# Attention, a gated layer and a rational layer in one kernel: sums of weights and tokens on GpSimd, the second layer's conversion spread over blocks 1 to 8, another order of VectorE's work in the pairs' stage

## The chip, the core and the metric

One core of a Trainium2 chip runs the whole program. The metric is the device time of one execution in microseconds, the median of several. TensorE (PE) multiplies, VectorE (DVE), ScalarE (ACT) and GpSimd (POOL) work on tiles, and SyncE (SP) issues nearly all transfers. Each engine, and SP's queue, works in the order in which the program issues to it.

## What is computed

Eight batches of eight heads attend over keys and values that are averaged in groups of eight; the result, 4608 tokens of 512 values, goes through a gated layer of 1536 hidden values, and then through a layer of 2048 with a rational function. In float32:

```
k_p, v_p = mean of k, v over 8 neighbours              # 576 -> 72 rows
x  = softmax(q @ k_p.T / 8) @ v_p                      # 4608 x 512
y  = (silu(x @ w_gate) * (x @ w_val)) @ w_out          # hidden 1536
h  = y @ w_in                                          # 2048
out = ((a0 + a1 h + a2 h^2 + a3 h^3) / (1 + |b0||h| + |b1| h^2 + 1e-6)) @ w_out2
```

## The kernel before

**Splitting.** A product in float32 is made of three products of rounded parts: every operand is split into a high part (ScalarE copies it into the rounded type) and a low part (VectorE subtracts the high part from the value). `split` (line 92) does both. The weights come as 64-bit numbers and are first converted to float32 in pieces: two ScalarE instructions (`words`), three VectorE ones and one integer addition on GpSimd (`bits`, lines 114 to 121), then the split.

**Stages.** Tokens are worked on in nine blocks of 512. The head does the attention of block 0. Blocks 0, 1 and 2 (the plain blocks, loop `for j in range(PLAIN)`) do the gated layer in 12 steps `f` of 128 hidden values: gate product, value product, their elementwise product, output product of the step before. In block 0 the first layer's weights are converted alongside. Then come three pairs of blocks (3 and 4, 5 and 6, 7 and 8), 36 steps `n`, in the pairs' stage. There Strassen's scheme takes 7 products of half-sized operands in place of 8 for the hidden values; a chain of banks `ca`, `cb`, `cc` accumulates them. The parts a11, s1, s2, a12, s3, s4, a22 of the weights are streamed from DRAM two steps ahead (`stream`), and the parts b11, t1, t2, b21, t3, b22, t4 of the tokens are made once per pair (`token_sums`, line 657, and `token_part`). The hidden values go to DRAM. A product stage then applies the output weights to the three pairs, again with 7 products (banks `ya`, `yb`, `yc`, line 1025), and the second layer runs over all nine blocks.

**Sums of the weights.** `weight_sums` runs in blocks 1 and 2, half a step's weights at a time: `whole` (line 607) adds the two parts of a weight, `sums` (612 to 615) makes four sums, `parts` splits them and stores them, all on VectorE and ScalarE. The same for the output weights is `out_load`, `out_sums` (803 to 810) and `out_parts`, in the steps of the third pair: two tiles of 512 KB are loaded back from DRAM per step, six VectorE instructions work on them, and 1 MB is split and stored.

**The second layer's weights.** `Halves` converts 64 pieces of 256 columns: `load`, then `step`, which starts one piece (ScalarE), finishes the one before it on VectorE and GpSimd, splits and stores the one before that. All of it stands in the pairs' stage. `rate(n)` gives the calls of `step` in step `n`: one and two in turn up to step 23, one up to 30, five from step 31 to 35.

**Order around the change.** The order is written out by hand. In a step of the pairs' stage TensorE does s1, s2, [place A: transposes of the attention], a22 of the step before (`end_chain`), a12, [place B: values], s4, a11 of the next step (`begin_chain`), s3, [place C: scores]. On VectorE the addition at line 876 stands behind `second.step()` and place A; the addition at 905 ends the step. TensorE's s4 needs the first, its a22 the second. `attention_slots` puts the attention of later blocks into these places: the softmax's scaling at line 372 and the copies of p at 383 run on GpSimd for pairs' blocks, and the transposes (line 400) need both. In block 2 these are the units of blocks 3 and 4, in steps 0 to 9. `prepare(2)` loads K and V pieces and reduces them at the end of the same step.

## Time and profile before

| | us |
|---|---|
| median of 3 runs | 1963.39 (1961.37 to 1963.74) |
| the profiled execution | 1963.66 |
| its span | 1961.9 |
| TensorE busy | 1813.9 |
| VectorE busy | 1484.3 |
| ScalarE busy | 1135.0 |
| GpSimd busy | 195.7 |

The span runs from the first to the last instruction of the profiled execution; the rows below are from that execution, with times counted from the span's start. By these times block 1 runs from 193 to 308 us, block 2 to 443, the pairs' steps from there to 953, the product stage to about 1155, and the second layer to the end. A wait in a view is idle time of an engine, put down to what released it; the chain follows the waits back from the last instruction.

### The profile page before, as it was taken

What the parts mean: (1) busy time and instruction counts of PE and PEld (TensorE: products, weight loads), DVE (VectorE), ACT (ScalarE), POOL (GpSimd) and SP (SyncE); (2) the same over time, 40 slices, a digit from 0 to 9 for tenths busy, and PEclk for the clock granted to TensorE, in tenths of its full rate; (3) what the DMA queues carried; (4) which work ended last, traced back from release to release, by engine and by line L of the source; (5) the groups of instructions that cost most, each with busy time, mean ns of one, the idle gap of its engine ahead of it and who ended that gap; (6) DMA issues with size and microseconds to landing.
All of it is one profiled execution on the core that took longest, in us unless ns stands there. A gap on an engine that the chain in (4) does not pass through costs nothing.

```text
span 1961.9 us, 23800 instructions
## 1 busy us (share of the span) xinstructions
PE 1813.9 (92%) x8212; PEld 1436.3 (73%) x8212; DVE 1484.3 (76%) x2563; ACT 1135.0 (58%) x1972; POOL 195.7 (10%) x258
## 2 busy tenths in 40 slices
PE   6889999998988998774899999999999999999998
PEld 5667777876776777653577778888888888888887
DVE  8997676675667556653676679898988888898987
ACT  5675345546555654332444467666767676766675
POOL 3563001201211220001000000000000000000000
PEclk9999999999999999987899999999999999999999
DMA  6521545477878777997972570101010010101000
GB/s 244 199 95 46 174 137 177 169 266 269 276 257 268 256 260 252 383 324 271 311 266 110 194 257 1 43 1 43 1 44 27 17 43 1 43 1 44 1 22 22
DMA packets 157464, 285.27 MB, mean 145 GB/s; under 512 B 12320, under 2 KB 78496, under 8 KB 156320
## 3 DMA queue, kind: packets, MB, share of 16 engines
q1 hardware_dynamic: 156192, 282.64, 41.9%
q8 instruction: 65, 1.06, 0.2%
q10 hardware_dynamic: 1152, 1.12, 0.2%
q14 instruction: 55, 0.45, 0.1%
HBM read 194.58 MB, written 89.13 MB: 145 GB/s over the span
## 4 chain that ended last, share of the span: by engine, by line
PE 67%; DVE 16%; DMA 9%; issue 4%; ACT 3%; SPq 1%; POOL 0%; POOLq 0%; ACTq 0%; DVEq 0%
PE acco L246 20%; PE h L246 20%; PE ca L246 5%; PE vp L246 4%; PE cc L246 3%; PE ya L1025 3%; PE acc L246 2%; PE gp L246 2%; DMA oo<-od 2%; PE cb L246 2%; PE pv L428 1%; PE yb L1025 1%; PE yc L1025 1%; DVE p L360 1%; DVE vp L293 1%
## 5 line engine op out<-in xcount | busy, mean ns | idle before, releaser
L246 PE MATMUL acco<-wo,gt 128*128 128x512 f32 x1728 | 426.6, 395 | 2.7 <-ACT gt L1112 2.2
L246 PE MATMUL h<-z,wi 128*128 128x512 f32 x1728 | 423.1, 393 | 0.8 <-ACT z L93 0.8
L246 PEld LDWEIGHTS acco<-wo,gt 128*128 128x128 f32 x1728 | 325.2, 188 | 80.6 <-ACT gt L1112 3.1
L246 PEld LDWEIGHTS h<-z,wi 128*128 128x128 f32 x1728 | 324.4, 188 | 77.0 <-ACT z L93 1.6
L1091 ACT ACTIVATE sq<-h 128x512 f32<-128x512 f32 x144 | 86.1, 598 | 221.4 <-PE h L246 221.3
L1098 DVE SCALAR_TENSOR_TENSOR w<-sq,neg,w 128x512 f32<-128x512 f32 x144 | 108.2, 751 | 66.7 <-ACT w L1092 62.2
L246 PE MATMUL gp<-x,wg 128*128 128x512 f32 x432 | 110.9, 404 | 10.3 <-POOL wg L149 10.3
L1108 DVE SCALAR_TENSOR_TENSOR g<-t,neg,e 128x512 f32<-128x512 f32 x144 | 108.3, 752 | 5.1
L1095 ACT ACTIVATE t<-h,neg 128x512 f32<-128x512 f32 x144 | 111.9, 777 | 0.0
L246 PE MATMUL vp<-x,wv 128*128 128x512 f32 x432 | 111.5, 406 | 0.3
L1104 DVE SCALAR_TENSOR_TENSOR t<-t,neg,h 128x512 f32<-128x512 f32 x144 | 107.7, 748 | 5.1
L246 PE MATMUL ca<-x2t,sw 128*128 128x512 f32 x216 | 62.5, 430 | 50.5 <-DVE cq L905 50.5
L1105 DVE SCALAR_TENSOR_TENSOR e<-w,ln 128x512 f32<-128x512 f32 x144 | 98.8, 686 | 13.5 <-ACT ln L1102 13.4
L246 PE MATMUL acc<-ht,wo 128*128 128x512 f32 x432 | 106.9, 396 | 0.4 <-ACT ht L732 0.4
L1102 ACT ACTIVATE ln<-ln,lnb 128x512 f32<-128x512 f32 x144 | 104.2, 724 | 4.7
L1106 DVE SCALAR_TENSOR_TENSOR e<-e,ln 128x512 f32<-128x512 f32 x144 | 99.7, 692 | 5.0
L246 PEld LDWEIGHTS gp<-x,wg 128*128 128x128 f32 x432 | 80.2, 190 | 31.4 <-POOL wg L149 13.0
L1112 ACT ACTIVATE gt<-g 128x512 fp32r<-128x512 f32 x144 | 91.0, 632 | 16.8 <-DVE g L1108 16.8
L1113 DVE TENSOR_TENSOR gt<-g,gt 128x512 fp32r<-128x512 f32 x144 | 98.9, 687 | 1.5 <-ACT gt L1112 0.8
L1092 ACT ACTIVATE w<-h,cab 128x512 f32<-128x512 f32 x144 | 98.3, 682 | 2.5 <-DVE e L1105 2.4
L1103 DVE TENSOR_TENSOR t<-t,h 128x512 f32<-128x512 f32 x144 | 98.3, 682 | 0.0
L246 PEld LDWEIGHTS vp<-x,wv 128*128 128x128 f32 x432 | 81.8, 194 | 20.1 <-POOL wv L149 2.1
(244 smaller groups left out, 3160.4 us busy)
## 6 DMA issues: line engine op xcount, KB each, us to landing
sw<-sd SPq DMA_DIRECT2D x72, 512.0 KB, 6.8
sw<-wd SPq DMA_DIRECT2D x36, 512.0 KB, 5.5
h<-hq SPq DMA_DIRECT2D x36, 512.0 KB, 3.5
sd<-sp SPq DMA_DIRECT2D x24, 512.0 KB, 3.2
sw<-vd SPq DMA_DIRECT2D x36, 256.0 KB, 7.2
hl<-h SPq DMA_DIRECT2D x18, 512.0 KB, 7.8
hr<-h SPq DMA_DIRECT2D x18, 512.0 KB, 9.9
out<-ob SPq DMA_DIRECT2D x36, 256.0 KB, 2.3
```

The source lines that it names most:

```text
L246: nc.tensor.matmul(acc, st[:, lw, cols], mv[:, rw, mcols], start=first and i == 0, stop=last and i == n - 1, skip_group_check=seeded,)
L1025: nc.tensor.matmul(banks[q], w[:, lw, cols], t[:, rw, :], start=opened and k == 0 and m == 0, stop=k == NK - 1 and m == 2, skip_group_chec ...
L1092: nc.scalar.activation(w0, hps, AF.Abs, scale=cab[:, 4:5])
L1095: nc.scalar.activation(t, hps, AF.Identity, scale=neg[:, 3:4], bias=neg[:, 2:3])
L1098: nc.vector.scalar_tensor_tensor(w0, sq, neg[:, 5:6], w0, op0=ALU.mult, op1=ALU.add)
L1102: nc.scalar.activation(ln, ln, AF.Exp, scale=-1.0, bias=lnb)
L1103: nc.vector.tensor_tensor(t, t, hps, op=ALU.mult)
L1104: nc.vector.scalar_tensor_tensor(t, t, neg[:, 1:2], hps, op0=ALU.add, op1=ALU.mult)
L1105: nc.vector.scalar_tensor_tensor(e, w0, C1, ln, op0=ALU.add, op1=ALU.mult)
L1106: nc.vector.scalar_tensor_tensor(e, e, 2.0, ln, op0=ALU.subtract, op1=ALU.mult)
L1108: nc.vector.scalar_tensor_tensor(g, t, neg[:, 0:1], e, op0=ALU.add, op1=ALU.mult)
L1113: lambda gt=gt, g=g: nc.vector.tensor_tensor(gt[:, 1, :], g, f32(gt[:, 0, :]), op=ALU.subtract),
```

## The change

- `split` can subtract on GpSimd. `weight_sums` does all its sums and its subtraction there; its store is issued at the next step.
- `out_load` goes. `out_sums` runs in block 2, steps 3 to 8, on the weights in SBUF, and `out_parts` and `out_store` follow, with sums and subtraction on GpSimd.
- `Halves` is cut into `begin`, `middle` and `end`: one piece is begun, converted, split (on GpSimd) in each step of blocks 1 and 2 and of the pairs, two in the last four steps, and stored at the next step's `begin`. Loads lead by one step. The pieces lie in three buffers of their own, in the pairs' stage in those of x too.
- `token_sums` and the sums of `hidden_part` in the product stage run on GpSimd.
- In a step of the pairs' stage the addition at line 876 is issued ahead of place A; `token_part` of t1 and t2 and the conversion come behind `end_chain`; the hidden values are stored one step later; K and V are reduced a step after they are loaded, ahead of place B.
- `vp` has one buffer in place of two, and the DMA scratch 1024 bytes in place of 4096.

```diff
-    def split(dst_hi, dst_lo, src):
+    def split(dst_hi, dst_lo, src, eng=None):
         nc.scalar.activation(dst_hi, src, AF.Copy)
-        nc.vector.tensor_tensor(dst_lo, src, f32(dst_hi), op=ALU.subtract)
+        (eng or nc.vector).tensor_tensor(dst_lo, src, f32(dst_hi), op=ALU.subtract)
...
+                i, self.n = self.n % 7, self.n + 1
+                if self.paired and i < KT:
+                    t = keep.tile([P, 2, BLK], F32R, tag=f"x{i}", name=f"raw{key}_{h}")
+                    t = t.rearrange("p t c -> p (t c)")
+                else:
+                    t = hp.tile([P, 768], F32R, tag="cv", name=f"raw{key}_{h}", bufs=3)
...
+        def store(self):
+            for key, h, w in self.after:
+                nc.sync.dma_start(self.kept[key][:, :, h * 256 : (h + 1) * 256], f32(w))
+            self.after = []
+
+        def begin(self, n=1, more=1):
+            self.store()
+            for _ in range(more):
+                self.load()
+            self.now = []
+            for key, h, tile_, raw in [self.raw.pop(0) for _ in range(min(n, len(self.raw)))]:
+                t = f32(tile_[:, 512:768])
                 words, bits, _ = conversion(f"{key}_{h}", raw, 256, True, t)
                 words()
+                self.now.append((key, h, tile_, t, bits))
...
+        def middle(self):
+            for x in self.now:
+                for fn in x[4]:
                     fn()
...
+        def end(self):
+            for key, h, tile_, t, _ in self.now:
+                w = tile_[:, :512].rearrange("p (t c) -> p t c", t=2)
+                split(w[:, 0, :], w[:, 1, :], t, nc.gpsimd)
+                self.after.append((key, h, w))
...
+                if c == 0:
+                    st["vp", b] = at.tile([P, NPAIR + 2, D], F32, tag="vp", name=f"vp{b}")
...
             for i, w in enumerate((g_w, v_w)):
-                nc.vector.tensor_tensor(r[:, i], cut(w, 0), cut(w, 1), op=ALU.add)
+                nc.gpsimd.tensor_tensor(r[:, i], cut(w, 0), cut(w, 1), op=ALU.add)
...
+            nc.gpsimd.tensor_tensor(t[:, 0], r[:, 1, 0], r[:, 1, 1], op=ALU.add)
+            nc.gpsimd.tensor_tensor(t[:, 1], t[:, 0], r[:, 0, 0], op=ALU.subtract)
+            nc.gpsimd.tensor_tensor(t[:, 2], r[:, 0, 0], r[:, 1, 0], op=ALU.subtract)
+            nc.gpsimd.tensor_tensor(t[:, 3], r[:, 0, 1], t[:, 1], op=ALU.subtract)
...
+            w = box["w"] = hp.tile([P, 2, 4, P], F32R, tag="sp", name=f"sp{f}_{kk}")
+            split(w[:, 0], w[:, 1], box["s"], nc.gpsimd)
...
+    def out_sums(k):
+        r = wslot(f"or{k}", (P, 2, 2, QUART), F32)
+        for i, f in enumerate((k, k + NF1 // 2)):
+            w = W1[f"o{f}"]
+            nc.gpsimd.tensor_tensor(
+                r[:, i].rearrange("p h c -> p (h c)"), f32(w[:, 0, :]), f32(w[:, 1, :]), op=ALU.add
+            )
+        t = o_box["s"] = wslot(f"os{k}", (P, 4, QUART), F32)
+        nc.gpsimd.tensor_tensor(t[:, 0], r[:, 0, 1], r[:, 1, 1], op=ALU.add)
+        nc.gpsimd.tensor_tensor(t[:, 1], t[:, 0], r[:, 0, 0], op=ALU.subtract)
+        nc.gpsimd.tensor_tensor(t[:, 2], r[:, 0, 0], r[:, 0, 1], op=ALU.subtract)
+        nc.gpsimd.tensor_tensor(t[:, 3], r[:, 1, 0], t[:, 1], op=ALU.subtract)
+
+    def out_parts(k):
+        t = o_box.pop("s")
+        w = o_box["w"] = [wslot(f"op{k}_{i}", (P, 4, QUART)) for i in range(2)]
+        split(*w, t, nc.gpsimd)
+
+    def out_store(k):
+        for i, w in enumerate(o_box.pop("w")):
+            nc.sync.dma_start(so_d[k][:, i], f32(w))
...
-                nc.vector.tensor_tensor(out[:, i, :], x[:, i, :], y[:, i, :], op=ALU.subtract)
+                nc.gpsimd.tensor_tensor(out[:, i, :], x[:, i, :], y[:, i, :], op=ALU.subtract)
...
             if j:
                 i = (j - 1) * NF1 + f
                 steps = weight_sums(i // 2, i % 2)
+                second.begin()
+            last_store()
             steps[0]()
...
+            if j:
+                second.middle()
+            if j == PLAIN - 1 and 3 <= f < 9:
+                out_sums(f - 3)
             place(j, f, "B")
...
             steps[2]()
+            if j:
+                second.end()
             place(j, f, "C")
             run()
             if j == PLAIN - 1:
                 nc.sync.dma_start(o_d[f], f32(W1[f"o{f}"]))
+                if 4 <= f < 10:
+                    out_store(f - 4)
+                if 3 <= f < 9:
+                    out_parts(f - 3)
...
-        run = prepare(2)
+        run = prepare(2, True)
...
-        if more:
-            token_part(p + 1, "t1")
+        second.begin(2 if n >= full_n - 4 else 1, 2 if n >= full_n - 6 else 1)
         part_product(bank_a[n], n, "s2", "t2", False)
-        if more:
-            token_part(p + 1, "t2")
-        ticks = rate(n)
-        second.step()
+        nc.vector.tensor_tensor(c, cq[n][:, 0, :], bank_a[n], op=ALU.add)
         place(stage, f, "A")
-        nc.vector.tensor_tensor(c, cq[n][:, 0, :], bank_a[n], op=ALU.add)
         if n:
             end_chain(n - 1)
         if f == 0 and p:
             token_part(p, "t4")
+        if more:
+            token_part(p + 1, "t1")
+            token_part(p + 1, "t2")
+        second.middle()
         stream(n + 2)
...
-        if ticks > 2:
-            second.step()
-        if p + 1 == len(PAIRS) and 1 <= f <= NF1 // 2:
-            out_sums(f - 1)
+        run()
         place(stage, f, "B")
...
-        if ticks > 1:
-            second.step()
-        if ticks > 3:
-            second.step()
+        if n > 0:
+            keep_hidden(n - 1)
+        second.end()
         place(stage, f, "B2")
...
-            if 1 <= f <= NF1 // 2:
-                out_parts(f - 1)
-            if f < NF1 // 2:
-                out_load(f)
...
         if sums:
-            nc.vector.tensor_tensor(src, *sums, op=ALU.subtract)
+            nc.gpsimd.tensor_tensor(src, *sums, op=ALU.subtract)
```

## Rows read from the trace of the kernel before

**Rows 1.** Page, part 2: busy tenths of TensorE in 40 slices

```profile
PE   6889999998988998774899999999999999999998
```

**Rows 2.** Busy time by stretch; the first line names the columns

```profile
core 0: us, PE busy (x) PEld busy (x) DVE busy (x) ACT busy (x) POOL busy (x), PEclk, DMA share, GB/s
308.00:442.90 134.90, 128.84 (x684) 101.52 (x678) 95.61 (x211) 69.93 (x110) 22.29 (x33) 1.00 0.61 207
442.90:610.50 167.60, 148.13 (x757) 118.72 (x758) 105.97 (x226) 92.41 (x172) 29.63 (x50) 0.94 0.80 267
610.50:766.70 156.20, 144.93 (x748) 116.45 (x747) 98.39 (x216) 93.32 (x172) 27.30 (x47) 0.98 0.76 250
766.70:854.60 87.90, 73.02 (x301) 56.58 (x301) 53.33 (x104) 30.16 (x58) 4.89 (x8) 0.98 1.02 371
854.60:943.30 88.70, 48.75 (x172) 37.20 (x171) 36.27 (x93) 30.17 (x77) 11.62 (x19) 0.77 0.80 267
```

**Rows 3.** Waits of PE, first two pairs (442.9 to 755.2): total us, times, longest

```profile
PE cc L246 <- DVE cc L876: 19.0, 5, 5.2
PE t L400 <- DVE p L360: 9.0, 8, 2.3
```

**Rows 4.** Waits of PE at the third pair's end (854.6 to 990)

```profile
PE ca L246 <- DVE cq L905: 41.5, 6, 17.2
```

**Rows 5.** Waits of ScalarE in the same stretch (854.6 to 957)

```profile
ACT rawo L110 <- DMA rawo<-in_wo: 27.9, 6, 9.8
ACT rawi L110 <- DMA rawi<-in_wi: 15.1, 6, 8.4
```

**Rows 6.** Chain that ended last, 755 to 990: start, us, what

```profile
818.29 7.37 DMA oo<-od
...
864.01 7.79 DMA rawo<-in_wo
...
989.50 8.30 PE yb L1025 x36
```

**Rows 7.** Timeline of PE, step 25: start us, us, instruction, count

```profile
780.73 1.52 PE L246 MATMUL cc<-x2b,sw 128*128 128x512 f32 x6
782.09 1.52 PE L246 MATMUL ca<-x2b,sw 128*128 128x512 f32 x6
```

**Rows 8.** Timeline of ScalarE: Silu of block 2, steps 3 and 9

```profile
335.47 0.60 ACT L722 ACTIVATE hh<-gp 128x512 f32<-128x512 f32 x1 [2.10 <-PE gp L246]
...
404.19 0.60 ACT L722 ACTIVATE hh<-gp 128x512 f32<-128x512 f32 x1 [2.14 <-PE gp L246]
```

**Rows 9.** GpSimd by line and shape: busy us, mean ns, idle before

```profile
L372 POOL TENSOR_TENSOR p<-p,sm 128x576 f32<-128x576 f32 x28 | 34.2, 1220 | 147.9 <-DVE sm L371 147.8
L117 POOL TENSOR_TENSOR rawi<-rawi 128x256 uint32<-128x256 uint32 x32 | 19.6, 612 | 199.6 <-DVE rawi L114 109.8 <-issue 33.0 <-ACT x2b L93 13.5
...
L149 POOL TENSOR_TENSOR wg<-rawg,wg 128x512 fp32r<-128x512 f32 x9 | 13.3, 1480 | 0.0
...
L322 POOL TENSOR_TENSOR vr<-vt,vr 32x256 fp32r<-32x256 f32 x8 | 5.8, 730 | 4.2 <-ACT vr L320 4.2
```

**Rows 10.** A group of VectorE in 308 to 443, same columns

```profile
L94 DVE TENSOR_TENSOR sp<-s,sp 128x512 fp32r<-128x512 f32 x12 | 7.9, 659 | 0.0
```

**Rows 11.** Timeline of VectorE and GpSimd in block 0, 54 to 59

```profile
54.45 0.69 DVE L114 SCALAR_TENSOR_TENSOR rawv<-rawv,tv 128x512 uint32<-128x512 uint32 x1
...
56.34 1.47 POOL L149 TENSOR_TENSOR wg<-rawg,wg 128x512 fp32r<-128x512 f32 x1
...
56.69 1.67 DVE L114 SCALAR_TENSOR_TENSOR rawo<-rawo,to 128x512 uint32<-128x512 uint32 x1
```

**Rows 12.** Timeline of GpSimd in block 2, step 3

```profile
334.76 0.47 POOL L383 COPY pr<-p 128x96 f32<-128x96 f32 x2
343.35 1.43 POOL L372 TENSOR_TENSOR p<-p,sm 128x576 f32<-128x576 f32 x1 [8.12 <-DVE sm L371]
344.84 0.47 POOL L383 COPY pr<-p 128x96 f32<-128x96 f32 x2
```

More of the change, by code (lines that the diff above doesn't have):

```diff
@@ L181, in __init__ @@
             self.todo = [(key, src, h) for key, src in items for h in range(2)]
-            self.raw, self.done, self.n = [], [], 0
+            self.raw, self.now, self.after, self.n, self.paired = [], [], [], 0, False
         def load(self):
@@ L186, in load @@
                 key, src, h = self.todo.pop(0)
-                i, self.n = self.n % 5, self.n + 1
-                pool, tag = (keep, f"x{i}") if i < KT else (hp, "sp")
-                tile_ = pool.tile([P, 2, BLK], F32R, tag=tag, name=f"raw{key}_{h}")
-                raw = tile_[:, 0, :].bitcast(U32).rearrange("p (n two) -> p n two", two=2)
-                nc.sync.dma_start(raw, src[:, h * 256 : (h + 1) * 256, :])
-                self.raw.append((key, h, tile_, raw))
-        def step(self):
-            self.done = self.done[-2:]
-            begun = None
-            if self.raw:
-                key, h, tile_, raw = self.raw.pop(0)
-                t = f32(tile_[:, 1, :256])
+                i, self.n = self.n % 7, self.n + 1
@@ new lines, in load @@
+                if self.paired and i < KT:
[3 more added lines that the diff above has]
+                    t = hp.tile([P, 768], F32R, tag="cv", name=f"raw{key}_{h}", bufs=3)
+                raw = t[:, :512].bitcast(U32).rearrange("p (n two) -> p n two", two=2)
+                nc.sync.dma_start(raw, src[:, h * 256 : (h + 1) * 256, :])
+                self.raw.append((key, h, t, raw))
@@ L624, in parts, with prepare @@
                 nc.sync.dma_start(v_d[f], f32(v_w[:, :, QUART:]))
-        return [whole, sums, parts]
-    todo = []
-    def prepare(n):
-        runs = [todo.pop(0)() for _ in range(min(n, len(todo)))]
+        return [whole, sums, parts, store]
+    o_box = {}
+    def out_sums(k):
[17 more added lines that the diff above has]
+            nc.sync.dma_start(so_d[k][:, i], f32(w))
+    todo = []
+    ready = []
+    def prepare(n, late=False):
+        runs = ready[:]
+        ready[:] = [todo.pop(0)() for _ in range(min(n, len(todo)))]
+        if not late:
+            runs, ready[:] = runs + ready, []
         def run():
@@ L710, in attention_gated_rational @@
             run = prepare(2)
-            steps = [lambda: None] * 3
+            last_store, steps = steps[3], [lambda: None] * 4
             if j:
@@ L749, in attention_gated_rational @@
             first.finish()
+            second.load()
         nxt = None
@@ L838, in left_load @@
         nc.sync.dma_start(t, h_d[p, k])
-    def rate(n):
-        if n < 2 * NF1:
-            return 1 + n % 2
-        return 1 if n < 2 * NF1 + 7 else 5
-    for _ in range(2):
-        second.load()
+    steps[3]()
+    second.paired = True
     begin_chain(0)
@@ L926, in attention_gated_rational @@
     end_chain(full_n - 1)
+    keep_hidden(full_n - 1)
     parts_x.clear()
     assert not plan and not todo and not any(sums_x.values())
-    while any(second.done[-2:]) or second.raw:
-        second.step()
+    second.store()
+    assert not second.todo and not second.raw
     ph1.close()
```

58 lines of the change are left out of this document (10 added, 48 removed).

## The prediction

> **What bounds the kernel now.** I read the slices first, then busy time by stretch, then the waits of each stretch, and last the chain, to learn which wait ends last. TensorE is busy nine tenths and more of nearly every slice; the exceptions are the head and the slices from about 780 to 980 us [rows 1]. The head isn't touched by the change. By stretch [rows 2]: block 2 (308.0 to 442.9) keeps PE at 128.8 of 134.9 us, the first two pairs (442.9 to 766.7) at 293.1 of 323.8 with the clock at 0.94 and 0.98, but the third pair falls to 73.0 of 87.9, then to 48.8 of 88.7 at clock 0.77. So the kernel is bound by TensorE except in the pairs' stage, and there mostly at its end.
>
> What ends PE's waits there: in the first two pairs the addition at line 876 (19.0 us) and the transposes of the attention (9.0 us, put down to line 360; they need GpSimd's p and pr) [rows 3]; at the end the addition at line 905, 41.5 us in six waits, one of 17.2 [rows 4]. These additions are late because VectorE runs in order behind something that waits for a transfer. From 780 to 854 us that is the reload of the output weights for `out_sums`: its link in the chain is some 7.4 us in every step. From 855 on it is the raw halves of the second layer [rows 6]; ScalarE waited 27.9 + 15.1 us for them [rows 5]. Up to 854 us the transfers are themselves the limit: 371 GB/s at a DMA share of 1.02 [rows 2].
>
> **Part 1, the third pair (from 766.7 to the first yb product at 989.5, 222.8 us).** The change moves the sums of the output weights to block 2, where the weights lie in SBUF, so 12 reloads of 512 KB and six stores of 1 MB leave. It also leaves one half of the second layer per step (two in the last four) in place of five per step. PE's floor: a product of six matmuls is issued every 1.36 us [rows 7], so a step of seven products takes 9.5 us and twelve take 114; one product of step 24 is done before the cut, -1.4, and three sets of 36 matmuls at 8.30 [rows 6] follow: 137.7. Bytes per step: weights streamed 1.84 MB, hidden values stored 0.52, a half loaded and stored 0.52, together 2.9 MB; at the 371 GB/s of [rows 2] that is 7.8 us, under 9.5. Not all of the 85 us comes back. The first token buffer of the product stage is the one that held the last half; it can be reused only when that half's store has landed, up to 7.8 us by the crowded transfer of [rows 6]. The last five steps carry 20.7 MB with the prefetches of the product stage, 56 us against 48, so some 8 us stay there. **Gain 70, between 55 and 78.**
>
> **Part 2, the first two pairs.** The addition at line 876 is now issued ahead of the transposes' evacuation and of the conversion, right behind the s2 product that it reads, so its 19.0 us go. The hidden store is put off by a step part, which frees SP's queue; the loads of K and V lead their reductions by one more step. PE idles 30.7 us in these stretches, and clocks of 0.94 over 167.6 and 0.98 over 156.2 cost 10 + 3 us of busy time [rows 2], as those dips come beside the idle time. At most 44. The transposes' 9 us are not sure to go: GpSimd gets the half's subtraction (0.4 us longer than on VectorE by lines 322 and 94, [rows 9, 10], the shapes scaled) ahead of the softmax product at 372. The bounds are 20 (the 19.0 alone, with little of the clock) and 44. As the idle time is what goes first, I take **32**. The token sums move from VectorE to GpSimd, eight instructions of at most 1.48 us [rows 9], 12 us in a step of about that length, read only in the next step: nothing, and 3 us each if ScalarE's rounding waits for a GpSimd addition behind them.
>
> **Part 3, block 2.** This is the cost. In steps 3 to 8 GpSimd gets, beside its attention work, two-operand work on 4864 elements per partition per step: 512 + 512 for the weights' sums, 512 for their low parts, 256 for the half's, 2048 for `out_sums`, 1024 for `out_parts`. The trace has such an instruction at 0.730 us for 256 elements (line 322) and 1.480 for 512 (149); the integer addition at 117 takes 0.612 for 256 [rows 9]. So 19 units of 256 take 11.6 us (at 0.612) to 14.1 (at 0.740). To these come the conversion's addition 0.61, the softmax product 1.22 [rows 9] and pr 0.47 [rows 12]: 13.9 to 16.4 us a step. I take 16.2, by line 322, the nearest form. A step takes (404.19 - 335.47)/6 = 11.45 us now [rows 8]. PE's transposes of step f+1 wait for pr, which stands behind all of step f in GpSimd's queue (today: product at 343.35, pr at 344.84, nothing between [rows 12]). So PE is paced by GpSimd: 6 x 4.75 = 28 us. Bounds: 14 (at 13.9), and 36 if VectorE's instructions hold GpSimd up by another 1.3 us a step. **Loss 28.** What VectorE no longer does in blocks 1 and 2 (the subtraction's 0.66 us [rows 10] and the six additions in front of it) gains nothing: PE is at 95% there.
>
> How row and rule meet here: beside a GpSimd subtraction of 1.47 us, VectorE's instruction at line 114, with two inputs in SBUF, took 1.67 us, where the same shape took 0.69 with GpSimd idle [rows 11]: it stood still until GpSimd was done. The Trainium skill, "SBUF — State Buffer", section "Who interferes with whom", says the same for VectorE instructions with two SBUF inputs: whichever comes second is fully blocked. The trace agrees for line 114. By this rule the block's loss would lie at its upper end, and the product stage would pay too (third rival). The skill's "GPSIMD Engine Reference", section 4.1, also names VectorE as the engine for elementwise work on a tile, which speaks against the change; the trace agrees on the price (1.48 against 0.66 us for 512 elements).
>
> **Part 4, the rest.** Blocks 1 and 2 get one half per step: 0.52 MB more in steps of 8.3 us (36 matmuls, [rows 6]) to 11.5, at 207 GB/s and a share of 0.61 in block 2 [rows 2], plus 1 MB of out_store per step in its second half; about 300 GB/s, below the 371 seen. On SP the half's store waits for GpSimd, and behind it stand a raw load and the weights' sums; K and V are issued ahead of it. Nothing, while loads lead by a step. One vp buffer makes the next V reduction wait for build_vs, steps earlier: nothing. The smaller descriptor scratch: the page lists no DMA that GpSimd issues, nothing. In the product stage GpSimd takes 72 sums; PE has seven buffers of lead: nothing. The second layer is unchanged.
>
> **Sum.** The profiled execution took 1963.66 (span 1961.9), the median 1963.39. 1963.7 - 70 - 32 + 28 = 1889.7; less the 0.3 to the median, 1889.
>
> **Rivals.** First, GpSimd is not the bound in block 2, as its queue drains while PE does its 11.45 us: 1861. For it: GpSimd is busy only 22.3 us in 134.9 [rows 2]; against: the sum of part 3. Second, transfers go on to bound the third pair, since the moved traffic is replaced by prefetches that still crowd the last five steps; half of its gain stays away: 1889 + 35 = 1924. For it the share of 1.02 [rows 2], against the 7.8 us of bytes per step. Third, the lock of [rows 11] acts everywhere: 36 in block 2 and, in the product stage, 24 sums x 1.48 + 42 subtractions x 0.66 = 63 us per pair against PE's 7 x 8.30 = 58, 15 us in all: 1912. Fourth, slower than before: the halves' loads, only one step ahead, come late in every step, and ScalarE, which converts them in order, stands in front of the Silu and the evacuations in 60 steps, as it does today in [rows 5]. A landing took up to 7.8 us in the crowd [rows 6] and a step of 36 matmuls takes 8.3. If SP's waits push it to 11 us, each step loses some 2.5: 1889 + 150 = 2039. It beats the gains from 1.25 us a step on.
>
> **How the numbers follow.** Forecast 0.60, first rival 0.12, second 0.12, third 0.10, fourth 0.06. The bounds give 1963 - 78 - 44 + 14 = 1855 to 1963 - 55 - 20 + 36 = 1924; the second rival lies at 1924, and I take 1855 to 1925. Only the fourth ends above; with its tail and that of the second (a loss in block 2 that grows beyond 36), faster by over 0.2% (what a measurement of this kernel can tell from none) 0.92, within 0.02, slower 0.06.
>
> **What would show it.** In the profile after: steps of the third pair of some 9.6 us and no chain link of oo; PE's wait on the line 876 addition near nothing and the clock at 1.00 in the pairs; GpSimd over 90% busy in block 2's steps 3 to 8, with steps of about 16 us and PE's transposes waiting for it; first yb product some 74 us earlier. Wrong it would be if block 2 keeps its 11.5 us steps, or if ScalarE waits for raw halves outside the last steps.

## The result and the profile after

| | before | after |
|---|---|---|
| median (lowest to highest), us | 1963.35 (1961.37 to 1963.74) | 1901.28 (1900.08 to 1901.61) |
| profiled execution, its span, us | 1963.66, 1961.9 | 1901.61, 1899.8 |
| ratio of after to before, 95% interval | | 0.9685 (0.9668 to 0.9701) |

The change made the kernel 3.15% faster. The forecast was 1889.0 in a range of 1855 to 1925: sign and range hold, and the likeliest value lies 12.3 us below the median. The profiled execution against the sum of the forecast, 1901.61 - 1889.7 = 11.9 us, can be taken apart by four cuts that both traces have: the first cq of the pairs (442.9 before, [rows 2]; 486.9 after), the cq that begins the third pair (766.7, [rows 2]; 775.9), the first yb product (989.3; the chain of [rows 6] has it from 989.5 on; 930.8 after) and the end of the span.

| stretch | before | after | measured | forecast |
|---|---|---|---|---|
| start to first cq (blocks 0 to 2) | 442.9 | 486.9 | +44.0 | +28 (14 to 36) |
| first two pairs | 323.8 | 289.0 | -34.8 | -32 (-20 to -44) |
| third pair to first yb | 222.6 | 154.9 | -67.7 | -70 (-55 to -78) |
| first yb to the end | 972.6 | 969.0 | -3.6 | 0 |
| sum | | | -62.1 | -74 |

So three of four terms came within 4 us, and one, the loss in block 2, was mis-sized by 16 and outside its own bounds. The slices of TensorE on the page of the kernel after, to be held against [rows 1], show both sides; GpSimd's slices and the granted clock stand with them:

```profile
PE   5889999878899999997999999999999999999998
...
POOL 2565766998123223212865400000000000000000
PEclk9989999889899999999999999999999999999999
```

A slice is 47.5 us. The hole of before in the slices from 780 to 980 us is gone but for one slice of 7. New ones of 8, 7, 8 and 8 stand at 333 to 523 us; in the first three of them GpSimd shows 9, 9 and 8, and the clock shows 8, 8, 9 and 8. By stretch, with the columns of [rows 2]:

```profile
339.30:437.30 98.00, 75.87 (x372) 58.73 (x371) 46.09 (x87) 50.03 (x80) 93.16 (x119) 0.88 0.61 213
437.30:461.90 24.60, 22.12 (x87) 17.93 (x88) 11.55 (x17) 7.35 (x17) 16.10 (x23) 0.86 0.75 258
461.90:486.90 25.00, 17.71 (x76) 13.47 (x74) 14.34 (x18) 11.87 (x23) 15.23 (x16) 0.86 0.74 254
486.90:775.90 289.00, 282.79 (x1508) 230.87 (x1508) 182.45 (x359) 174.56 (x310) 89.78 (x127) 0.99 0.80 273
775.90:930.80 154.90, 141.81 (x602) 113.68 (x602) 82.64 (x123) 61.52 (x127) 50.52 (x50) 0.97 1.01 350
```

The first row runs from the Silu of block 2's step 3 to that of step 9. It answers to [rows 8], where the same six steps took 68.7 us: +29.3. GpSimd is busy 93.16 of 98.0 us, the fifth busy column, TensorE 75.87 at a granted clock of 0.88. The second row, from there to the Silu of step 11, the last, is 5.0 longer than before (19.6), all of it between the Silus of steps 9 and 10. The third, from the last Silu to the first cq, is 5.9 longer (19.1). The remaining 3.8 us of the 44.0 lie ahead of the Silu of step 3. The fourth row is the first two pairs, at clock 0.99 in place of 0.94 and 0.98 [rows 2]; the fifth is the third pair, at 0.97 in place of 0.77 at its worst.

What TensorE waited for in block 2 (300 to 487 us) of the kernel after; us in total, times, longest:

```profile
PE t L416 <- POOL pr L395: 20.9, 8, 3.8
PE ca L256 <- ACT ys L822: 6.5, 1, 6.5
PE t L412 <- POOL p L384: 5.2, 4, 1.9
```

These are the transposes of the attention, which need GpSimd's pr and p, and once the first product of the tokens' stage. The timeline of step 5 shows why pr is late; start us, us, instruction, in brackets the idle time before it and its releaser:

```profile
370.06 2.34 POOL L94 TENSOR_TENSOR op<-os,op 128x1024 fp32r<-128x1024 f32 x1
372.35 0.47 POOL L395 COPY pr<-p 64x96 f32<-64x96 f32 x2
...
372.66 0.47 PE L416 MATMUL t<-ident,pr 64*96 64x64 f32 x2 [2.01 <-POOL pr L395]
...
385.69 2.34 POOL L94 TENSOR_TENSOR op<-os,op 128x1024 fp32r<-128x1024 f32 x1
```

The copy pr stands right behind the subtraction of `out_parts`, the last work of the step before. Before, nothing stood between product and copy [rows 12]. The next such subtraction begins 15.6 us later. GpSimd's groups in these six steps; line, operation and shape, count, busy us, mean ns, idle before:

```profile
L647 POOL TENSOR_TENSOR or<-wo 128x512 f32<-128x512 f32 x12 | 16.0, 1353 | 0.0
L94 POOL TENSOR_TENSOR op<-os,op 128x1024 fp32r<-128x1024 f32 x6 | 14.0, 2338 | 0.0
L94 POOL TENSOR_TENSOR sp<-s,sp 128x512 fp32r<-128x512 f32 x7 | 8.9, 1276 | 0.0
...
L619 POOL TENSOR_TENSOR r<-wv 128x256 f32<-128x256 f32 x6 | 4.4, 729 | 0.0
...
L624 POOL TENSOR_TENSOR s<-r 128x128 f32<-128x128 f32 x6 | 3.1, 510 | 0.5
...
L117 POOL TENSOR_TENSOR rawo<-rawo 128x256 uint32<-128x256 uint32 x3 | 1.8, 607 | 0.0
```

The 256 elements of line 619 cost 0.729, the same as line 322 in [rows 9], from which the forecast took its price. Per step GpSimd was busy 93.16 / 6 = 15.5 us, against 16.2 forecast.

The end of block 2, from the timeline:

```profile
460.27 2.60 POOL L700 TENSOR_TENSOR t<-xraw,xraw 128x512 f32<-128x512 f32 x2
...
474.35 0.63 ACT L93 ACTIVATE sp<-s 128x512 fp32r<-128x512 f32 x1 [8.24 <-POOL s L627]
...
477.94 2.92 PE L256 MATMUL ca<-x0b,sw 128*128 128x512 f32 x6 [6.48 <-ACT ys L822]
```

The token sums (line 700; the row is two of eight) stand in GpSimd's queue ahead of the last weights' sums (line 627). ScalarE stood 8.24 us for those, and behind it waited its evacuations (ys), for which TensorE stood 6.48 us.

In the first two pairs (486.9 to 775.9) the waits of [rows 3] have shrunk. These are TensorE's longest there:

```profile
PE cc L256 <- DVE cc L897: 5.4, 2, 4.9
PE ca L256 <- DVE cq L927: 1.7, 1, 1.7
```

Line 897 is the old 876 (19.0 us in [rows 3]), line 927 the old 905 (41.5 us in [rows 4], in the third pair). The longest of the five waits of [rows 3], 5.2 us in the first step of the pairs' stage, has not gone: it is the 4.9 here.

The wait that is left in front of the product stage, on TensorE's timeline, with the two sets of products behind it:

```profile
901.25 10.93 PE L1041 MATMUL ya<-h0b,oa 128*128 128x512 f32 x36 [8.82 <-ACT h0b L93]
912.02 8.76 PE L1041 MATMUL yc<-h0t,os 128*128 128x512 f32 x36
...
920.62 10.32 PE L1041 MATMUL ya<-h0t,os 128*128 128x512 f32 x36
```

ScalarE itself waited there for the store of the last half, from whose buffer it wanted to make h0b:

```profile
ACT h0b L93 <- DMA o_parts<-rawo: 8.5, 1, 8.5
```

### The profile page after: what moved, and what is told of

Read it like the earlier page. It is cut to its first block, busy times and chain, and to the rows that moved or that the text cites. A ratio compares the mean times of both kernels' runs of the same rounds, so it can differ in the third digit from the quotient of the medians.

```text
span 1899.8 us, 23844 instructions
## 1 busy us (share of the span) xinstructions
PE 1795.7 (95%) x8212; PEld 1437.7 (76%) x8212; DVE 1431.6 (75%) x2193; ACT 1132.2 (60%) x1972; POOL 550.6 (29%) x628
## 4 chain that ended last, share of the span: by engine, by line
PE 53%; DVE 3%; DMA 1%; issue 1%; ACT 0%; SPq 0%; DVEq 0%; ACTq 0%
PE acco L256 21%; PE h L256 21%; PE ya L1041 4%; PE ca L256 3%; PE yc L1041 2%; PE cc L256 1%; PE cb L256 1%; DMA sw<-wd 1%; PE yb L1041 1%; DVE h2t L94 0%; DVE h1t L94 0%; DMA hl<-h 0%; DVE h1b L94 0%; DVE h0b L94 0%; DMA o_parts<-rawo 0%
## 5 line engine op out<-in xcount | busy, mean ns | idle before, releaser
L256 PE MATMUL vp<-x,wv 128*128 128x512 f32 x432 | 123.7, 440 | 0.2
L1121 DVE SCALAR_TENSOR_TENSOR e<-w,ln 128x512 f32<-128x512 f32 x144 | 98.7, 685 | 13.5 <-ACT ln L1118 13.4
L256 PEld LDWEIGHTS vp<-x,wv 128*128 128x128 f32 x432 | 91.3, 216 | 22.9 <-POOL wv L149 1.5
L256 PEld LDWEIGHTS gp<-x,wg 128*128 128x128 f32 x432 | 80.5, 191 | 29.8 <-POOL wg L149 11.3
L256 PEld LDWEIGHTS acc<-ht,wo 128*128 128x128 f32 x432 | 80.4, 188 | 18.3
```

The costliest lines, as they stand in the source:

```text
L256: nc.tensor.matmul(acc, st[:, lw, cols], mv[:, rw, mcols], start=first and i == 0, stop=last and i == n - 1, skip_group_check=seeded,)
L1121: nc.vector.scalar_tensor_tensor(e, w0, C1, ln, op0=ALU.add, op1=ALU.mult)
```

## Experiments

Each variant changes the kernel after, and was timed beside the kernel before on the same chip. The last column is the ratio less 0.9685, times 1963 us, which takes the differences between chips out. The intervals of two ratios together leave about 5 us of it open; where less counts, the stretches of the profiles are compared.

| variant | median, us | ratio to before (95% interval) | against after, us |
|---|---|---|---|
| e1 out_sums on VectorE | 1899.01 | 0.9681 (0.9662 to 0.9699) | -1 |
| e9 pr copied early | 1893.29 | 0.9636 (0.9616 to 0.9656) | -10 |
| e10 e1 and e9 | 1884.91 | 0.9595 (0.9577 to 0.9612) | -18 |
| e5 out_sums back in the third pair | 1887.30 | 0.9623 (0.9606 to 0.9639) | -12 |
| e2 token sums on VectorE | 1896.45 | 0.9646 (0.9627 to 0.9664) | -8 |
| e6 no halves in blocks 1 and 2 | 1909.80 | 0.9718 (0.9702 to 0.9734) | +6 |
| e3 buffers of the halves turned by one | 1892.61 | 0.9652 (0.9637 to 0.9666) | -6 |
| e4 order of the pairs' stage back | 1910.77 | 0.9738 (0.9721 to 0.9754) | +10 |
| e11 K and V lead by one step less | 1903.61 | 0.9692 (0.9678 to 0.9707) | +1 |
| e12 halves' low parts on VectorE | 1894.36 | 0.9645 (0.9631 to 0.9659) | -8 |
| b6 out_sums in the second pair | 1867.93 | 0.9514 (0.9494 to 0.9533) | -34 |
| b6g the same on GpSimd | 1878.59 | 0.9564 (0.9549 to 0.9580) | -24 |

### What paces block 2: e1, e9, e10

**e1** puts the six sums and differences of `out_sums` back on VectorE (their place in block 2 stays).

```diff
-            nc.gpsimd.tensor_tensor(
+            nc.vector.tensor_tensor(
                 r[:, i].rearrange("p h c -> p (h c)"), f32(w[:, 0, :]), f32(w[:, 1, :]), op=ALU.add
...
-        nc.gpsimd.tensor_tensor(t[:, 0], r[:, 0, 1], r[:, 1, 1], op=ALU.add)
+        nc.vector.tensor_tensor(t[:, 0], r[:, 0, 1], r[:, 1, 1], op=ALU.add)
...
```

> The six additions of out_sums go back to VectorE, still in block 2; all else as in the changed kernel. Theory (GpSimd's queue paces block 2 from step 3 to 9): in the changed kernel these six take GpSimd some 5.8 us of its 15.6 per step (or 2 x 1.26, os 0.74 + 1.07 + 0.73 + 0.72), so about 10 are left, under the 11.5 us that PE needs; VectorE gets 3 us and stays under PE too. Steps 3 to 8 return to 11.5 to 12 us, the block ends some 30 us earlier, time about 1870. Rival (the stores of out_parts and of the halves, or SP's queue, pace the block): bytes are the same, so steps stay over 14 us and the time over 1893.

Measured: 1899.01, no difference from after that can be told. The six steps of block 2 in e1, as a row of the windows, and what GpSimd waited for in them:

```profile
341.30:435.30 94.00, 76.62 (x372) 59.24 (x370) 63.97 (x123) 49.44 (x79) 63.18 (x81) 0.89 0.64 222
```

```profile
POOL p L384 <- DVE sm L383: 23.7, 6, 5.8
```

GpSimd is busy only 63 of 94 us, 30 less than in after, and the steps are still 94.0 / 6 = 15.7 us long. The theory that its sum alone paces the block falls. Now GpSimd itself waits, 23.7 us in six waits, for the sums of the softmax on VectorE. This is a loop over the engines: pr is issued at the start of the next step behind all of GpSimd's work, the transposes wait for pr, VectorE's softmax comes behind its own sums (1.81 us for the two of line 647 in this trace), the product on GpSimd behind the softmax, and the three subtractions behind the product again stand in front of pr. Transfers, the rival's limit, don't set it, although the time lies in the rival's range: their share is 0.64, and neither TensorE, VectorE, ScalarE nor GpSimd waits for one in these steps. The loop is read from these waits and from TensorE's for pr (18.8 us from 300 to 480); e10 tests it.

**e9** leaves the sums on GpSimd and copies pr a step part earlier, right behind the softmax product.

```diff
             put(slot + 1, "B2", lambda u=u: box["s", u][2]())
-            put(slot + 2, "0", lambda u=u: box.pop(("s", u))[3]())
+            put(slot + 1, "B2", lambda u=u: box.pop(("s", u))[3]())
```

> One line: GpSimd's copies pr are issued behind the softmax product of the same step (place B2), ahead of the three low-part subtractions, and not at the next step's start. All GpSimd work stays. Two things can pace block 2's steps: GpSimd's sum of work (93.2 us busy in 98.0, 15.5 a step), or the loop pr, transposes, VectorE, softmax product, subtractions, pr. Theory (the sum paces it): only the 4.4 us of subtractions that PE need not wait for in the last of the steps are won, 3 to 8 us in all, 1893 to 1898. Rival (the loop alone): the loop is 4.4 us shorter in each of six or seven steps, 25 us are won, about 1876.

Measured: 1893.29. The same six steps in e9:

```profile
332.80:430.80 98.00, 74.98 (x376) 59.51 (x376) 56.81 (x87) 50.14 (x80) 93.41 (x118) 0.88 0.60 213
```

The loop is cut, and the steps are as long as in after, with GpSimd 95% busy. So with all the work on GpSimd its sum does pace the block. The 10 us come from elsewhere: the window begins 6.5 us earlier, and 4.3 are won behind it, between the Silus of steps 9 and 10.

**e10** is both edits together.

> Both: the six additions of out_sums on VectorE and pr issued behind the softmax product. With the additions on VectorE alone GpSimd was busy only 63.2 us of 94.1 and the steps still took 15.7. Theory (then the loop pr, transposes, VectorE's work with 4.9 us of additions in it, softmax product, 4.4 us of subtractions paces the steps): with the subtractions out of the loop 15.7 - 4.4 = 11.3 us are left, PE's own pace; block 2 wins 22 to 27 us, time 1873 to 1880. Rival (transfers or SP's queue pace the steps): no change, 1897 to 1901.

Measured: 1884.91, 18 below after, but 5 to 12 above the time that the theory gave. The six steps in e10, then what TensorE waited for in them, then the timeline of one place:

```profile
336.00:425.60 89.60, 74.17 (x372) 58.03 (x372) 75.93 (x123) 49.58 (x79) 64.96 (x81) 0.92 0.66 234
```

```profile
PE t L412 <- DVE p L372: 11.0, 5, 3.2
```

```profile
365.50 2.37 POOL L94 TENSOR_TENSOR op<-os,op 128x1024 fp32r<-128x1024 f32 x1
...
366.60 2.80 DVE L120 TENSOR_SCALAR rawi<-rawi 128x256 f32<-128x256 f32 x1
...
367.83 0.73 POOL L619 TENSOR_TENSOR r<-wg 128x256 f32<-128x256 f32 x1
368.53 0.72 POOL L619 TENSOR_TENSOR r<-wv 128x256 f32<-128x256 f32 x1
```

Steps of 14.9 us, with GpSimd at 65 of 89.6 and VectorE now at 76. Part of what VectorE counts as busy is standing still. The view of line 120 in e10 gives shortest, median and longest of this instruction in ns:

```profile
L120 DVE TENSOR_SCALAR rawi<-rawi x7: 287/1618/2801, 306.2 to 475.2; 128x256 f32<-128x256 f32 x7
```

It takes 0.29 us when nothing is in its way, and 2.80 when it begins beside a GpSimd subtraction of 2.37 us with two of line 619 right behind: it ended at 369.40, when the second of them had ended (369.25). TensorE's wait for pr is gone, as the loop would have it, but the steps are only 0.7 us shorter than in e1, where the theory had 4.4. So removing two limits uncovers a third, VectorE held up by GpSimd: the windows of e1 and e10 both hold 123 of VectorE's instructions, and they are busy 63.97 us in the one and 75.93 in the other, 2.0 us more per step. How much of that reaches TensorE, whose wait is now for VectorE's part of p, was not taken apart.

### What the moved sums cost and brought: e5, e2, e6

**e5** takes the sums of the output weights out of block 2 and puts reload, sums and parts back in the third pair, on VectorE; all else is as after.

```diff
-            if j == PLAIN - 1 and 3 <= f < 9:
-                out_sums(f - 3)
...
-                if 4 <= f < 10:
-                    out_store(f - 4)
-                if 3 <= f < 9:
-                    out_parts(f - 3)
...
         run()
+        if p + 1 == len(PAIRS) and 1 <= f <= NF1 // 2:
+            out_sums(f - 1)
...
+            if 1 <= f <= NF1 // 2:
+                out_parts(f - 1)
+                out_store(f - 1)
+            if f < NF1 // 2:
+                out_load(f)
```

> The sums of the output weights go back into the third pair, reloaded from DRAM and done on VectorE as before the change; the halves, the order and the other GpSimd work stay as in the changed kernel. Theory: block 2 loses its GpSimd load of 8 us a step and some 35 to 40 us go there; in the third pair six steps carry 2.1 MB more each, 5.0 MB at 371 GB/s or 13.4 us in place of 9.5, 20 to 24 us more. Time 1880 to 1890: the move itself cost more than it brought, and the third pair's gain came from the halves. Rival (the reloads were what held the third pair): it grows by 45 or more, time over 1905.

Measured: 1887.30. Block 2's six steps and the third pair in e5:

```profile
339.70:407.60 67.90, 66.61 (x370) 53.32 (x370) 42.70 (x87) 43.85 (x73) 46.80 (x76) 1.00 0.68 231
...
740.90:917.70 176.80, 150.84 (x601) 119.08 (x601) 106.64 (x165) 67.11 (x133) 51.00 (x50) 0.91 1.03 373
```

Without these sums the steps of block 2 are back at 11.3 us, TensorE at 98% and the clock at 1.00; GpSimd's other new work hides. The first cq comes at 453.0, 33.9 us earlier than in after. The third pair is 176.8 - 154.9 = 21.9 us longer. So this one move cost 34 and brought 22, near what the theory had. The other 46 of the 67.7 us gained in the third pair came with the rest of the change.

**e2** puts only the token sums back on VectorE.

```diff
-                nc.gpsimd.tensor_tensor(out[:, i, :], x[:, i, :], y[:, i, :], op=ALU.subtract)
+                nc.vector.tensor_tensor(out[:, i, :], x[:, i, :], y[:, i, :], op=ALU.subtract)
```

> The sums of the tokens go back to VectorE. Theory: at the end of block 2 GpSimd's eight subtractions (10.7 us) stand ahead of step 11's weight sums, so ScalarE waits 8.2 us for those and PE 6.5 us for ScalarE; with the sums on VectorE (5.2 us in the trace of before) that wait goes and nothing else changes: 1901 - 5 to 7, about 1895. Rival (VectorE's own delay at the block's end, as before the change, takes its place): within 2 us of 1901.

Measured: 1896.45. TensorE's wait at the end of block 2 in e2, to be held against the 6.5 above:

```profile
PE ca L256 <- ACT ys L822: 0.9, 1, 0.9
```

The boundary (last Silu to first cq) takes 19.8 us in place of 25.0. The token sums on GpSimd cost some 5 us; the 8 by the ratios don't contradict that, with 5 of them open.

**e6** converts no halves in blocks 1 and 2; the pairs' steps then take one and two by turns, two in the third pair and three in the last steps.

```diff
-                second.begin()
+                pass
...
-            if j:
-                second.middle()
...
-            if j:
-                second.end()
...
+    RATE = [1 + n % 2 for n in range(24)] + [2] * 8 + [3] * 4 + [0]
...
-        second.begin(2 if n >= full_n - 4 else 1, 2 if n >= full_n - 6 else 1)
+        second.begin(RATE[n], RATE[n + 1])
```

> No half of the second layer is converted in blocks 1 and 2; in the pairs' steps one and two in turn up to step 23, as before the change, then two in steps 24 to 31 and three in the last four. The order in the step and all GpSimd work stay. With the order undone the time rose by only 9.5 us, all in the steps where a pair ends, so 25 of the 35 us won in the first two pairs have another cause. Theory (the even rate of one half per step): the steps with two halves grow by 1 to 3 us again, 12 to 25 us in the first two pairs, while block 2 wins some 5; the third pair carries 3.9 MB in the last steps and grows by 5 to 10. Time 1910 to 1930. Rival (the lead of K and V, or the store of hidden values put off): the first two pairs stay within 4 us of 289.

Measured: 1909.80. The first cq comes at 472.6, 14.3 us earlier; the first two pairs take 292.0, 3.0 more; the third pair 173.7, 18.8 more. Its largest wait, TensorE's in front of the product stage in e6:

```profile
PE ya L1038 <- ACT h0b L93: 16.8, 1, 16.8
```

So spreading the halves cost 14 us in blocks 1 and 2 and bought 22 later: it pays, but by some 7 net, and nearly all that it brings lies in the third pair. The time lies where the theory had it, but not by the theory's way, which had 12 to 25 in the first two pairs. These hardly felt two halves in every second step, as the rival had it; whether by the rival's cause, this run doesn't say. Nor does it bring back the old rate in the third pair (five in each of the last five steps), so the 18.8 need not be all that the new rate is worth there.

### The first two pairs and the last wait: e4, e11, e12, e3

**e4** puts the old order of one stretch back: t1, t2 and the conversion ahead of the addition, the addition behind place A.

```diff
+        if more:
+            token_part(p + 1, "t1")
         part_product(bank_a[n], n, "s2", "t2", False)
-        nc.vector.tensor_tensor(c, cq[n][:, 0, :], bank_a[n], op=ALU.add)
+        if more:
+            token_part(p + 1, "t2")
+        second.middle()
         place(stage, f, "A")
+        nc.vector.tensor_tensor(c, cq[n][:, 0, :], bank_a[n], op=ALU.add)
```

> In the pairs' stage the addition behind s2 stands again behind the conversion's VectorE work and place A, and the token parts t1 and t2 stand ahead of it, as before the change; all else as in the changed kernel. Theory (the order took away the waits of the first two pairs): PE's waits for that addition return, about 19 us with the clock's part up to 30; time 1916 to 1931. Rival (the even rate of the halves and the longer lead of K and V took them away): within 5 us of 1901.

Measured: 1910.77, between the two. The first two pairs in e4, and TensorE's waits in front of the product that needs the addition:

```profile
487.60:784.60 297.00, 284.30 (x1503) 232.08 (x1504) 186.50 (x362) 175.12 (x311) 89.00 (x127) 0.98 0.79 268
```

```profile
PE cc L256 <- DVE cc L903: 7.6, 4, 2.8
PE cc L256 <- ACT p L378: 5.9, 1, 5.9
```

297.0 in place of 289.0: the order is worth 8 of the 34.8 us. The 5.9 is the wait of the first step, which after has too (4.9); the two rows together are 13.5 us, against 19.0 in [rows 3] and 5.4 in after. So the order accounts for 8 of the 14 us that went from this wait. Part of the rest stood behind the token sums, which VectorE no longer does. In the kernel before, in step 10:

```profile
579.96 1.28 DVE L657 TENSOR_TENSOR t<-xraw,xraw 128x512 f32<-128x512 f32 x2
...
586.10 0.69 DVE L876 TENSOR_TENSOR cc<-cq,ca 128x512 f32<-128x512 f32 x1
```

TensorE waits 4.6 us for that addition in step 10 and 3.8 in step 22, where the token sums stand too; in e4, with these sums on GpSimd, it waits 1.1 in each. The two were not undone together.

The times of the cq show where the 34.8 us lie. The last two steps of each pair (10, 11, 22, 23) took 60.0 us before, 41.0 in after and 51.5 in e4: 19.0 of the gain lie there, and there the order counts. The other 16 lie in steps like step 4, which took 15.7 us before and 11.5 in after, and took 11.5 in e4 as well.

**e11** reduces K and V in the step in which they are loaded, as before.

```diff
-        run = prepare(2, True)
+        run = prepare(2)
...
-        run()
         place(stage, f, "B")
...
         place(stage, f, "C")
+        run()
```

> K and V are reduced again in the step that loads them, behind place C, as before the change; all else as in the changed kernel. In the trace of before the transposes waited 9.0 us for line 360, the softmax's subtraction, which stands behind these reductions and behind low parts that wait for ScalarE (VectorE waited 31.9 + 28.8 us for those in the first two pairs). Theory (the reductions' place): the transposes wait again, 10 to 20 us in the first two pairs, 1911 to 1921. Rival (the low parts of the halves on VectorE were the cause): 5 us or less, under 1906.

Measured: 1903.61, within the uncertainty of after; the first two pairs take 291.2. The extra lead is worth 2 us there.

**e12** gives the halves' low parts back to VectorE.

```diff
-                split(w[:, 0, :], w[:, 1, :], t, nc.gpsimd)
+                split(w[:, 0, :], w[:, 1, :], t)
```

> The low parts of the halves are subtracted on VectorE again, at their new place; all else as in the changed kernel. Theory (VectorE's wait for ScalarE's high part, in front of the softmax's sum, made the first two pairs slow): these grow by 10 to 20 us, while block 2 wins some 4 us from GpSimd's queue: 1907 to 1917. Rival (what counts is that the three pieces of a half are spread over the step, so that ScalarE is done when VectorE comes to it): the first two pairs stay within 3 us of 289 and the time falls to 1894 to 1899.

Measured: 1894.36, faster than after, as the rival had it; the first two pairs take 286.2, and the first cq comes 6.2 us earlier, behind the blocks in which GpSimd has less to do. VectorE's waits in them, in e12:

```profile
DVE rawi L94 <- ACT rawi L93: 34.4, 11, 5.0
DVE rawo L94 <- ACT rawo L93: 29.9, 10, 5.0
```

The kernel before has the same two waits in its first two pairs:

```profile
DVE rawo L94 <- ACT rawo L93: 31.9, 10, 5.9
DVE rawi L94 <- ACT rawi L93: 28.8, 9, 6.1
```

VectorE stands 64 us for ScalarE's high parts, and TensorE hardly feels it: its waits for VectorE in these pairs are 6.3 us in all, against 7.1 in after. The addition is issued ahead of that wait now. So this suspect for the 20 us and more that are left falls, at least alone.

**e3** turns the numbering of the halves' buffers by one, so that the last half doesn't lie in the buffer that the product stage takes first.

```diff
-                i, self.n = self.n % 7, self.n + 1
+                i, self.n = (self.n + 6) % 7, self.n + 1
```

> The buffers of the halves are counted from six in place of zero, so that the last half lies in a buffer of its own and not in x0, the first buffer of the product stage. Theory: the 8.8 us that PE waits ahead of the first ya product (ScalarE waits 8.5 us for the store of the last half) go; time about 1893. Rival (the wait is set by the loads of the hidden values and of the output weights, and only lands on the store): ScalarE waits for another transfer, 2 us or less are won, 1899 to 1902.

Measured: 1892.61, and TensorE's wait in front of the product stage, 8.8 us in after, is gone in e3:

```profile
PE ya L1041 <- ACT h0b L93: 0.4, 1, 0.4
```

The third pair takes 147.4 us, 7.5 less than in after.

### A better place for the sums: b6, b6g

e5 says that the sums are bought too dearly in block 2, and that in the third pair transfers are the limit (share 1.03). The first two pairs have room in both: a share of 0.80 and VectorE busy 182.45 of 289.0 us in after. **b6** reloads the output weights in the second of them, one pair of tiles every second step, with sums and low parts on VectorE, and takes e2 and e3 along.

```diff
         run()
+        if p == 1 and f % 2:
+            out_sums(f // 2)
...
+        if p == 1:
+            if f % 2:
+                out_parts(f // 2)
+                out_store(f // 2)
+            else:
+                out_load(f // 2)
```

> Three changes at once: the sums of the output weights are reloaded and done on VectorE in the second pair, one set in every two steps; the token sums on VectorE; the last half in a buffer of its own. By the single runs: block 2 wins 34 us as with the sums in the third pair, the token sums 5 and the buffer 9, while the second pair, with 2.1 MB and 4.3 us of VectorE's work more in every second step (273 GB/s before), loses 3 to 10: 1857 to 1866. Should the second pair's transfers or VectorE's order hold PE up, it is 1870 and more.

**b6g** is the same with the sums and low parts of the output weights on GpSimd.

> As the run before, with the six additions and the low parts of the output weights on GpSimd. GpSimd gets 8 us in every second step beside 3.7; if its sum paces the steps, as in block 2, 11.7 us are under the 12 us of a step and nothing is lost, but the softmax product stands behind 5.6 us of additions: 0 to 2 us lost in six steps. Time 1855 to 1868.

Measured: 1867.93 and 1878.59, 2 and 11 us above the ranges expected. The first two pairs and the third in b6:

```profile
446.90:745.20 298.30, 283.38 (x1508) 230.40 (x1508) 210.97 (x416) 180.77 (x317) 74.40 (x111) 0.99 0.88 307
745.20:894.40 149.20, 144.23 (x600) 113.44 (x601) 83.28 (x124) 61.67 (x127) 50.12 (x49) 0.98 0.99 345
```

and the same in b6g:

```profile
449.00:761.00 312.00, 291.24 (x1519) 236.10 (x1520) 192.43 (x378) 180.97 (x316) 114.45 (x152) 0.97 0.84 293
761.00:905.10 144.10, 139.36 (x590) 109.23 (x590) 80.73 (x119) 61.89 (x127) 52.47 (x50) 1.00 1.00 357
```

Against after, b6's first cq is 40.0 us earlier, its first two pairs 9.3 longer, its third pair 5.7 shorter: 36.4 in all, of 35.6 by the spans. The reload that the change removed, put where share and VectorE have room, costs some 12 us: the first two pairs take 287.8 in e2 and the third 147.4 in e3, whose edits b6 has too, and in b6 they take 298.3 and 149.2. Block 2's way without any reload cost 34. On GpSimd the same work costs some 9 us more in the three pairs (312.0 + 144.1 against 298.3 + 149.2). b6 is 4.9% faster than before and 1.8% faster than after (0.9514 / 0.9685).

## Why the prediction was right or wrong

**Part 1, right.** The floor of 137.7 us, some 8 us of crowding in the last steps and the wait for the last half's buffer gave 152.8; 154.9 came. The steps have no chain link of oo, the stretch no wait like that of [rows 4], and the buffer's wait, put at up to 7.8 by [rows 6], was 8.8. e3 shows it to be that buffer. That the sum came out is in part luck, as two of its terms are off by about as much in opposite directions. The eleven steps up to the last cq took 107.3 us, where 11 x 9.52 = 104.7 are the floor, so crowding cost 2.6 there and not 8. The three sets of 36 matmuls at 8.30 each were to take 24.9; from 901.25 to 930.78 they took 29.5, and they took 30.5 in e3, which doesn't have the wait in front of them. That transfers stay near their limit and yet don't pace TensorE was right as well: 350 GB/s at a share of 1.01, TensorE at 92%. The second rival is out.

**Part 2, right in size by luck, only partly in cause.** 34.8 against 32, the clock at 0.99 where 1.00 was forecast. But the forecast let the order of VectorE's work carry at least 20 us, all 19.0 of [rows 3] and a little of their clock, and e4 makes it 8; 5 of the 19.0 are still there. The lead of K and V is worth 2 (e11), the rate of the halves 3 (e6), their low parts on GpSimd less than nothing (e12: -2.8). These single undoings leave more than 20 us unexplained, 16 of them in steps that are as short in e4 as in after. Each leaves the others in place; two or three of them undone together, for instance the old order with the low parts behind ScalarE or the token sums on VectorE, were not tried. Nor was the store of the hidden values put back to its old place, which the forecast named as one of the causes. The cause of the 20 us and more stays open.

**Part 3, the term that was mis-sized.** The mechanism and the price per step were right: 15.5 us of GpSimd work against 16.2, GpSimd over 90% busy, the transposes waiting for pr, and +29.3 us in six steps against 28. GpSimd's queue carries its lag on behind the Silu of step 9 (+5.0), and by e5 33.9 us hang on `out_sums` and `out_parts` with their stores, still inside the bounds of 14 to 36. What took the loss to 44.0 and out of the bounds are places for which the forecast had put nothing: the boundary behind the block (+5.9), where e2 gives some 5 to the token sums, and the steps ahead of step 3 (+3.8). There the halves are a suspect, as in e6, without them in blocks 1 and 2, the Silu of step 3 comes at 335.5, as in [rows 8]. One execution of each kernel doesn't prove it: with the halves it lies between 332.8 (e9) and 341.3 (e1).

"GpSimd's sum" was not the only limit of that length, either. e9 shows the sum (93.41 us busy in six steps of 98.0). The waits of e1 point to a loop through pr of the same length (94.0 us with GpSimd busy 63.18), so that lifting one leaves the other; e10, which lifts both, took the wait for pr away and met a third.

**The token sums, wrong.** Part 2 put them at "nothing, and 3 us each if ScalarE's rounding waits for a GpSimd addition behind them". The condition came true with a larger price: 8.24 us of ScalarE, 6.48 of TensorE, some 5 us of time by e2. Named as read only in the next step, they were thought harmless; but what stands behind them in GpSimd's queue is read at once.

**Part 4, right but for blocks 1 and 2.** 3.6 us less from the first yb on; the sums in the product stage cost nothing there that shows in the time. The halves in blocks 1 and 2, put at nothing, cost 14 us by e6. Some 8 of these lie in the six steps (98.0 against 89.6 us), where part 3 had counted them in GpSimd's sum; the others no part had. In the first two pairs no half's transfer is among ScalarE's waits; in front of the product stage there is the one for the last store.

**The rivals.** The first (GpSimd hides in block 2, 1861) fell by the step length. The third (the lock everywhere, 1912) fell in the product stage, where 15 us were expected and 3.6 were gained. Its time came nearer than the forecast's, but not by its way. In block 2 the lock is real: e10's line 120, at 2.80 against 0.29 us, shows it, as [rows 11] did for line 114. The Trainium skill, "SBUF — State Buffer", section "Who interferes with whom", names `tensor_scalar` among those that can take the pair of ports shared with GpSimd, with the later one fully blocked; the trace of e10 agrees. How much of the 44 us is the lock can't be told. In the six steps 87 of VectorE's instructions are busy 46.09 us in after and 42.70 in e5, so VectorE is held some 3 us more there, and GpSimd's sum can cover that. The fourth (ScalarE in front of late halves, 2039) didn't occur.

## What to carry to other kernels

Work moved to an idle engine has to be added up per step with what that engine already does, and followed past the last step in which it is issued: what stands behind it in the queue pays, too. When an engine is nearly full, look for a second limit of the same length, a loop that runs through several in-order engines, before expecting a gain from unloading it. And a transfer saved is worth only what it costs where it would lie: the same reload took 22 us where transfers were at their limit and some 12 where they had room.

## What the runs showed of the hardware

GpSimd's subtractions and additions of two fp32 inputs took, by the medians of after in blocks 1 and 2, 0.46 us for 128 elements per partition (0.57 in line 626), 0.73 to 0.74 for 256, 1.28 to 1.32 for 512 and 2.34 for 1024, so that a large one is a fifth cheaper per element than the 0.73 for 256 that the forecast took. In the product stage the 72 of line 979, with 512 elements, took 1.73 to 1.74 us by the median, though the shortest of them took 1.27; no run shows what held them, and TensorE's waits from 940 us on name no instruction of GpSimd. And a VectorE instruction of 0.29 us, begun beside a subtraction of GpSimd that ended at 365.50 + 2.37 = 367.87, was held until 369.40, through two more GpSimd instructions.
